# Opening order of the score and transpose steps, seeded product chains and a split last chain in a fused local-attention and squared-ReLU kernel

## The chip, the cores and the metric

The kernel runs on one core of one Trainium2 chip. The metric is the device time of one execution in microseconds (us), lower is better. Three runs of the kernel before took 202.9, 204.08 and 204.08 us; the median is 204.08 us.

## What is computed

Attention over four batches, eight heads, 768 positions and head size 64, in which a query sees the 96 latest keys and the 8 first ("global") ones, with a bias that falls with distance by a slope of its own for each head. Its output, 3072 rows of 512, goes through a two-layer network with a squared ReLU.

```python
scores = (1/8) * q @ k.T                              # per batch and head
keep   = (pos_k < 8) | ((rel >= 0) & (rel < 96))      # rel = pos_q - pos_k
dist   = where(global and not local, 96, |rel|)
a      = softmax(where(keep, scores - slope[h] * dist, -1e9))
x      = (a @ v) rearranged to (3072, 512)
out    = relu(x @ w_in) ** 2 @ w_out                  # w_in 512 x 2048, w_out 2048 x 512
```

## The kernel before, in words

**Tiles and halves.** A tile is 128 rows of one batch; six tiles make a batch, three a "half", so there are eight halves. For a tile, TensorE multiplies its queries with the keys of its own tile ("o") and with those of the tile before plus the 32 first keys ("b"). ScalarE (ACT) takes the exponential, VectorE (DVE) multiplies by a mask that holds bias and window, TensorE multiplies with v (whose 65th column of ones gives the sum), DVE divides, and the result is turned to x, columns by rows, for the first layer. In the first layer (`hps`) a job multiplies one block of 128 hidden units with the 384 rows of a half. In the second layer a pair of tiles from `layer2_pair` is multiplied by seven products instead of eight, from sums and differences of activations and weights (`token_sum`, `weight_sum`); part of the first layer does the same in `layer1_group`.

**Who decides the order.** The program lists jobs and hands them to a planner (`Plan`), a list scheduler with costs written by hand. TensorE's jobs keep the order in which they are listed, and so do the loads that GpSimd (POOL) issues. DVE and ACT operations are placed by the planner, by readiness and by `RANKS`, and then stand in a fixed order on their engine: an instruction that waits holds up everything behind it on that engine. A PSUM bank is given to a TensorE job by the planner, and comes free when its last reader is done.

**The opening** (batch 0, halves 0 and 1) is listed by hand in `OPENING` (line 20). `T r` turns q and k of tile r: eight transposes into one bank, waiting for both loads, then one copy of each; `T0` does tiles 0 and 1 in two banks. `S r o` and `S r b` are the scores of tile r. For tiles 0 to 2 the bias is added by TensorE itself: `score_tile` (line 1207) first multiplies eight scaled identities (`slope_id`) with the distance table `dmask16`, and then adds the eight products of q and k in the same two banks, so the exponential gives the weights directly (tile `ph`). `A r i` multiplies the weights with v for two pairs of heads, `X r i` turns the result to x. `V r` copies v of tile r into `vb`, with the first 32 rows replaced by the global keys; `kb` is the same for k. `F`, `G`, `E`, `D` are first-layer jobs on one, two, two and one tiles; the digit is the quarter of w_in that they need. `LOADING` (line 26) is the order of POOL's loads: q, k, v of tile r and the quarters c0 to c3 of w_in. q and k of tiles 0 and 1 come by another way: SP and ACT issue four plain loads to `y` buffers, which DVE and ACT cast.

**Fillers.** `warm` (line 274) lets TensorE multiply zeros, or turn a block of zeros, where the planner sees spare time in the first 24 us. On a bank that is to hold transposes the filler is a transpose and needs `ident`; on another it is an ordinary product of zeros.

**Chains of a pair.** In `layer2_pair` (line 1012) the products p1 and p2 make one sum, p1, p6, p7, p4 run through bank "a", p5 and p3 through "f", p2 through "c". Between them partial sums are copied out (`keep`) and added (`give`). For the last pair of all, the order is p1 p5 p6 p2 p7 p3, and then `last_part` (line 1127) does p4 in two halves of 128 columns in the same bank, each with its own copy and store.

## Time and profile before

| | |
|---|---|
| three runs | 202.9, 204.08, 204.08 us |
| the profiled execution, its own time | 203.4 us |
| its span, first to last instruction | 201.6 us |
| TensorE busy | 194.4 us (96%), 2292 products |
| weight loads of TensorE | 160.2 us (79%) |
| DVE busy | 174.6 us (87%) |
| ACT busy | 144.7 us (72%) |
| POOL busy | 67.0 us (33%) |

The profile is of one execution. Times are counted from the first instruction. "Busy" of TensorE (PE) includes the fillers and overlaps of pipelined products, so it isn't a measure of useful work. A wait is written as the engine and line that waited, an arrow, and what ended the wait. A line number can be that of a helper: L264 is every DVE copy, L262 every ACT copy, L393 every load of q, k or v. The granted TensorE clock is at full speed from 6.7 us after the start to the end.

### The profile page before, as it was taken

Reading aid. Unit: us, or ns where it says so; the run is one execution under the profiler, and the core shown is the slowest. Engines: PE = TensorE matmul, PEld = TensorE weight load, DVE = VectorE, ACT = ScalarE, POOL = GpSimd, SP = SyncE. Lnnn points to the kernel's source line nnn. Section 1 sums busy time; section 2 is a strip of 40 time slices with the busy share of each in tenths; the row PEclk is TensorE's granted clock in tenths of the full one; section 3 lists DMA queues with packets and bytes.
Section 4 is the critical chain, followed back from the end, with each engine's and each line's share of the span. In section 5 each row is a group of like instructions: output and inputs, shape, how many; then the busy total and the mean of one; then the engine's idle time right before and its main releaser. Section 6 shows DMA issues by size and latency. Waiting matters only on the chain.

```text
span 201.6 us, 5781 instructions
## 1 busy us (share of the span) xinstructions
PE 194.4 (96%) x2292; PEld 160.2 (79%) x2292; DVE 174.6 (87%) x456; ACT 144.7 (72%) x304; POOL 67.0 (33%) x82
## 2 busy tenths in 40 slices
PE   6797999999999999999999999999999999999993
PEld 6676898975797776788888878987788788987883
DVE  7679999999997699899999999989899979288922
ACT  6797989699621998978988897658886952368220
POOL 7995648169007900950491039200000000000000
PEclk9999999999999999999999999999999999999999
DMA  6999999999998998999899969995212022200123
GB/s 160 177 150 191 198 180 154 197 207 165 169 182 137 197 186 161 107 184 120 191 152 162 174 139 147 176 148 160 41 53 75 3 76 90 82 25 0 52 105 106
DMA packets 106491, 27.12 MB, mean 134 GB/s; under 512 B 96992, under 2 KB 103520, under 8 KB 106464
## 3 DMA queue, kind: packets, MB, share of 16 engines
q0 software_dynamic: 74944, 13.11, 86.2%
q1 hardware_dynamic: 30320, 13.05, 30.8%
q10 hardware_dynamic: 1200, 0.59, 1.1%
q8 instruction: 18, 0.29, 0.6%
q14 instruction: 9, 0.07, 0.1%
HBM read 27.26 MB, written 6.29 MB: 166 GB/s over the span
## 4 chain that ended last, share of the span: by engine, by line
PE 87%; DVE 4%; DMA 3%; POOL 3%; ACT 1%; issue 0%; POOLq 0%
PE yps L1025 33%; PE hps L701 27%; PE hps L804 13%; PE sp L594 4%; PE av L655 4%; PE yps L948 3%; DMA v<-in_v_dram 3%; DVE tm L1285 1%; POOL v L393 1%; POOL w_mix L393 1%; DVE vb L264 1%; PE trp L531 1%; PE av L1271 1%; DVE kb L264 1%; PE yps L1132 0%; POOL sk L393 0%
## 5 line engine op out<-in xcount | busy, mean ns | idle before, releaser
L701 PE MATMUL hps<-xt,w_in_sb 128*128 128x384 f16 (+2 forms) x432 | 62.5, 290 | 0.0
L701 PEld LDWEIGHTS <-w_in_sb 128*128 128x128 f16 x432 | 37.2, 98 | 12.1
L726 ACT ACTIVATE hr<-hps 128x384 f16<-128x384 f32 (+1 forms) x74 | 37.4, 517 | 8.5 <-PE hps L701 7.6
L262 ACT COPY y<-yps 128x256 f32<-128x256 f32 (+2 forms) x40 | 15.4, 384 | 31.3 <-PE yps L1025 26.7
L1025 PEld LDWEIGHTS <-h 128*128 128x128 f16 x344 | 32.9, 98 | 4.7
L607 ACT ACTIVATE ex<-sp 128x512 f16<-128x512 f32 x66 | 34.7, 621 | 2.7 <-PE sp L594 2.6
L393 POOL DMA_DIRECT2D sk<-in_k_dram x19 | 17.2, 914 | 51.6 <-DMA q<-sq 44.5
L1025 PEld LDWEIGHTS <-mixed 128*128 128x128 f16 x264 | 25.3, 98 | 3.4
L1080 DVE TENSOR_TENSOR y<-yps,y 128x256 f32<-128x256 f32 x33 | 13.8, 418 | 12.5 <-PE yps L1025 6.7
L393 POOL DMA_DIRECT2D v<-in_v_dram x24 | 21.6, 923 | 2.9 <-DMA w_in_sb<-in_moe_w_in_dram 1.6
L1025 PE MATMUL yps<-w_out_sb,h 128*128 128x256 f16 x176 | 21.9, 273 | 0.0
L1025 PE MATMUL yps<-w_mix,h 128*128 128x256 f16 x168 | 21.8, 273 | 0.0
L1025 PE MATMUL yps<-w_mix,mixed 128*128 128x256 f16 x176 | 21.7, 273 | 0.0
L631 DVE TENSOR_TENSOR phat<-ex,mask 128x1024 f16<-128x1024 f16 (+1 forms) x36 | 20.7, 592 | 0.1
L262 ACT COPY kept<-hps 128x384 f32<-128x384 f32 x30 | 13.4, 484 | 6.5 <-PE hps L804 6.4
L393 POOL DMA_DIRECT2D sq<-in_q_dram x19 | 16.9, 911 | 3.1 <-DVE rec L1283 1.7
L862 DVE TENSOR_TENSOR hr<-hps,kept 128x384 f16<-128x384 f32 x33 | 17.4, 547 | 0.6 <-ACT kept L262 0.3
L804 PEld LDWEIGHTS <-in_mix 128*128 128x128 f16 x176 | 14.9, 98 | 1.9
L740 ACT ACTIVATE h<-hr 128x768 f16<-128x768 f16 (+1 forms) x20 | 15.5, 775 | 0.4
L742 DVE TENSOR_TENSOR h<-hr 128x768 f16<-128x768 f16 (+1 forms) x28 | 13.9, 500 | 1.2 <-ACT hr L726 1.1
L804 PE MATMUL hps<-x_mix,in_mix 128*128 128x192 f16 x132 | 14.6, 246 | 0.0
L665 DVE TENSOR_TENSOR tm<-av,rec 128x384 f16<-128x384 f32 x24 | 13.4, 557 | 0.9
(108 smaller groups left out, 336.8 us busy)
## 6 DMA issues: line engine op xcount, KB each, us to landing
out_dram<-y SPq DMA_DIRECT2D x23, 256.0 KB, 2.4
v<-in_v_dram POOLq DMA_DIRECT2D x24, 128.0 KB, 7.1
sq<-in_q_dram POOLq DMA_DIRECT2D x19, 128.0 KB, 6.5
sk<-in_k_dram POOLq DMA_DIRECT2D x19, 128.0 KB, 5.9
w_in_sb<-in_moe_w_in_dram POOLq DMA_DIRECT2D x4, 512.0 KB, 11.1
w_out_sb<-in_moe_w_out_dram POOLq DMA_DIRECT2D x4, 512.0 KB, 10.1
y<-in_k_dram ACTq DMA_DIRECT2D x2, 256.0 KB, 4.9
y<-in_q_dram SPq DMA_DIRECT2D x2, 256.0 KB, 4.3
```

The costliest lines, as they stand in the source:

```text
L262: nc.scalar.copy(out=out, in_=in_)
L393: dma = nc.gpsimd.dma_start(out=dst, in_=src[x.b, :, r0 + t * P:r0 + (t + 1) * P, :] .rearrange("h p d -> p h d"))
L607: nc.scalar.activation(out=st["ex"][:, h], in_=sp[h], func=AF.Exp, scale=scale)
L631: eng(e).tensor_tensor(out=x.phat[a][:, :, t0:t0 + n], op=ALU.mult, in0=st["ex"][:, :, i0:i0 + 2 * n].rearrange("p e (t b) c -> p e t (b c ...
L701: nc.tensor.matmul(st["ps"][:, i * n:(i + 1) * n], lhsT=w_in_sb[:, kk, m * P:(m + 1) * P], rhs=x.xt[:, kk, c0:c1], start=kk == 0, stop=kk ...
L726: nc.scalar.activation(out=o, in_=i, func=AF.Relu)
L740: nc.scalar.activation(out=h2, in_=hr, func=AF.Square)
L742: eng(e).tensor_tensor(out=h2, in0=hr, in1=hr, op=ALU.mult)
L804: nc.tensor.matmul(st[name][:, i * HC:(i + 1) * HC], lhsT=left(i, kk), rhs=right(kk), start=fresh and i == kk == 0, stop=kk == KK - 1, ski ...
L862: eng(e).tensor_tensor(out=hidden(which)[:, :, cols], in0=sums(name), in1=st[kept], op=ALU.add)
L1025: nc.tensor.matmul(st[bank_name][:, 0:HN], lhsT=a(m), rhs=b(m), start=fresh and m == 0, stop=m == HK - 1, skip_group_check=not fresh)
L1080: eng(e).tensor_tensor(out=y, in0=ps, in1=y, op=ALU.add)
```

## The change

1. **Opening.** The bias products of tiles 0 to 2 become jobs of their own (`P r o`, `P r b`, function `distances`); `score_tile` then adds the products of q and k to the banks that these jobs took. `T r` of tiles 2 to 5 is split into `Q r` and `K r`, each with one load to wait for, four transposes, a bank of its own and one copy. `T0` and `T1` are now the two halves of what `T0` was. `OPENING` is a new order of all of it, and begins with two bias jobs; `LOADING` has a new order, too.
2. **Seeds.** Where `SEEDS` (one half of the first layer) or `PAIR_SEEDS` (three pairs of tiles) say so, the order of the seven products is p1 p5 p6 p3 p7 p2 p4: after p3 has been read out of bank "f", the sum that p1 left is copied back into that bank (`seed`), and p2 adds to it there, so p2's result is only copied or put through the ReLU instead of being added by DVE.
3. **The last pair.** Its chain p1, p6, p7, p4 runs in two banks, "a0" and "a1", each with 128 of the 256 columns: eight jobs of eight products of half the width in place of three of full width and two of half width. The last store of each half stays with SP and ACT.
4. **Constants of the planner.** `PLACES`, `MIX`, `RANKS`, `LAYER1`, `FIRST`, `KEEP`, `SHY` are changed, so jobs of the later halves stand in another order; `WIDE` does the token sums of five pairs in one piece instead of seven; `BY_DMA` makes the two v copies of the last half by DMAs that SP issues. A copy of k after its transposes comes after that of q, and the priority of some operations on ACT is changed.

```diff
-OPENING = """T0 T2 S0o S1o S2b V1 S1b A00 T3 V2 A01 S2o A10 S3o A11 A21 T4 X11 X01 S3b A20 X00 T5 X21 S4o
-X20 X10 F1 S4b A31 G11 V3 G10 G01 F0 A41 X31 A30 G00 S5b A40 F3 X30 G30 F2 X41 V4 X40 S5o
-G21 E10 E00 E11 A50 G20 A51 X50 G31 X51 E01 D0 D1"""
+OPENING = """P0o P1b T0 T1 K3 S0o K2 P1o S1b S1o Q2 A00 A01 P2b S2b P2o Q3 A10 Q5 S2o X01 A11 Q4 S3o K4
+V1 X10 A20 A21 X00 X11 S4o K5 S3b X20 X21 F1 S4b S5o G10 G11 F0 V3 V2 S5b V4 A30 G01 A40 G00
+A41 A31 X30 F3 G30 X40 X31 X41 G21 A51 A50 E11 F2 G20 G31 X51 E10 X50 E00 D0 E01 D1"""
...
-LOADING = """v1 q2 k2 k3 q3 v0 v2 q5 q4 k4 k5 c1 v3 c0 v4 c3 c2 v5"""
+LOADING = """v1 k3 k2 q3 q2 v0 q4 q5 v2 k5 k4 c1 v3 c0 v4 c3 v5 c2"""
...
-PLACES = {2: (4.0, 8.4, 10.0, 10.1, 14.3, 14.1, 0, 0, 0, 0),
...
-SHY = 0.25
-MIX = [88, 46, 22, 0, 32, 54]
-BY_DMA = [0, 0, 0, 0, 0, 0, 0, 0]
-WIDE = [1, 1, 1, 0, 1, 1, 1, 1, 0, 0, 0]
+SHY = 0.3
+MIX = [114, 48, 26, 84, 10, 70]
+BY_DMA = [0, 0, 0, 0, 0, 0, 0, 1]
+SEEDS = [0, 0, 1, 0, 0, 0, 0, 0]
+PAIR_SEEDS = [0, 0, 0, 0, 0, 1, 1, 0, 1, 0, 1]
+WIDE = [1, 1, 0, 1, 0, 0, 1, 1, 0, 0, 0]
...
-LAYER1 = {2: "ssasbsscdssessfsssg", 3: "asbcsdessfABCsgDEssFsG",
...
+LAYER1 = {2: "ssasssbsscdsesssfgs", 3: "sabcsdseAfBsCsgDEsFssG",
...
-FIRST = [0, 0, 0, 1, 2, 5, 2, 1]
-KEEP = [0, 1, 2, 1, 7, 3, 2]
+FIRST = [0, 0, 0, 1, 5, 3, 4, 1]
+KEEP = [0, 1, 2, 1, 7, 4, 3]
...
+            if seeded:
+                give(run("f", False, weight(1, 0), plain(1, 0), [ops["seed"]]), "f", 0, 0)
+            else:
+                give(run("c", True, weight(1, 0), plain(1, 0)), "c", 0, 0, "keep1")
...
-            give(job, "f", 0, 1, "keep2")
+            added = give(job, "f", 0, 1, "keep2")
+            if not seeded:
+                return
+
+            def seed(e):
+                copy(e, sums("f"), st["keep1"])
+            ops["seed"] = plan.after(job, {"ACT": 0.41, "DVE": 0.48}, seed, [added, ops["keep1"]])
+            ops["seed"].shy = {"DVE": SHY}
+            bufs["keep1"].used_by(ops["seed"])
...
+            (p1, p5, p6, p3, p7, p2, p4) if seeded else (p1, p2, p5, p6, p3, p7, p4))]
...
+            if seeded:
+                job = run("f", False, plain(x, i, 1), weight(1, 0), [ops["seed"]])
+            else:
+                job = run("c", True, plain(x, i, 1), weight(1, 0))
             x.h2_buf.used_by(job)
-            give(job, "c", 0, 0, "keep1")
+            give(job, "f" if seeded else "c", 0, 0, None if seeded else "keep1")
 
         def p5():
...
+            if seeded:
+                def seed(e):
+                    copy(e, st["f"][:, 0:HN], part(0, 0))
+                ops["seed"] = plan.after(job, {"ACT": 0.31, "DVE": 0.36}, seed,
+                                         [st["done", 0][-1], ops["keep1"]])
+                ops["seed"].shy = {"DVE": SHY}
+                y_bufs[0].used_by(ops["seed"])
 
...
-        def last_part(c):
-            cols = slice(c * HN // 2, (c + 1) * HN // 2)
-
-            def emit(e):
-                for m in range(HK):
-                    nc.tensor.matmul(st["a"][:, cols], lhsT=z.h2[:, HK + m, j * P:(j + 1) * P],
-                                     rhs=mixed_weights[0][:, 3, m, cols], start=False, stop=m == HK - 1,
-                                     skip_group_check=True)
-            job = plan.pe(HK * (HN / 4800 + 0.003), emit,
-                          [*plain(z, j, 1)[1], *mix_ops[3], ops["c22"]])
-            job.users = st["users", "a"]
-            job.users[0].append(job)
-
-            def move(e):
-                copy(e, part(1, 0)[:, cols], st["a"][:, cols])
-            op = plan.after(job, {"ACT" if c else "DVE": 0.25}, move)
...
+        def first_chain(step, c):
+            name = f"a{c}"
+            if step == 1:
+                if "s" not in st:
+                    st["s"], st["ops"] = mix_tokens(one, two)
+                job = run(name, True, plain(x, i, 0), weight(0, 0))
+                x.h2_buf.used_by(job)
+                keep(job, name, "keep1")
+            elif step == 6:
+                job = run_mixed(name, False, 1, mixed_weight(1), [ops[f"keep1{c}"]])
+                keep(job, name, "keep2")
+            elif step == 7:
+                job = run_mixed(name, False, 2, mixed_weight(2), [ops[f"keep2{c}"]])
+                give(job, name, 1, 1, "keep5")
+                ops["c22", c] = st["done", 1][-1]
+            else:
+                job = run(name, False, plain(z, j, 1), mixed_weight(3), [ops["c22", c]])
+                give(job, name, 1, 0)
+
         cost = HK * (HN / 2400 + 0.003)
         if final:
-            return [(cost, f) for f in (p1, p5, p6, p2, p7, p3)] + [
-                (cost / 2, lambda c=c: last_part(c)) for c in range(2)]
-        return [(cost, f) for f in (p1, p2, p5, p6, p3, p7, p4)]
+            def halves_of(step):
+                return [(cost / 2, lambda c=c: first_chain(step, c)) for c in range(2)]
+            return [*halves_of(1), (cost, p5), *halves_of(6), (cost, p2), *halves_of(7),
+                    (cost, p3), *halves_of(4)]
+        return [(cost, f) for f in ((p1, p5, p6, p3, p7, p2, p4) if seeded else
+                                    (p1, p2, p5, p6, p3, p7, p4))]
...
+    def turn_first(which):
+        st = first_turn
 
         def emit(e, pairs, fresh):
-            for i, src in enumerate((x.sq, x.sk)):
-                if fresh and i < n:
+            for i, src in enumerate((x0.sq, x0.sk)):
+                if fresh:
                     st[i] = bank([P, 2, NPAIR, P], FP16, "trp0", i)
                     if i == 0:
-                        warm(st[0].rearrange("p i a c -> p (i a c)"))
+                        warm(st[0].rearrange("p j a c -> p (j a c)"))
                 for a in pairs:
-                    for j in range(n):
-                        nc.tensor.transpose(out=st[i * (n - 1)][:, i if n == 1 else j, a, :],
-                                            in_=src[:, t + j, 2 * a:2 * a + 2, :], identity=ident)
-        if n == 1:
-            job = plan.pe(0.56, lambda e: emit(e, range(NPAIR), True),
-                          [x.q_in[t], x.k_in[t], ident_op], 1)
-        else:
-            half = plan.pe(0.56, lambda e: emit(e, (0, 1), True), [*first[::2], ident_op], 2)
-            job = plan.pe(0.56, lambda e: emit(e, (2, 3), False), first[1::2])
-            job.users = half.users
-            for u in job.users:
-                u.append(job)
-
+                    for j in range(2):
+                        nc.tensor.transpose(out=st[i][:, j, a, :], in_=src[:, j, 2 * a:2 * a + 2, :],
+                                            identity=ident)
...
+        if which == 0:
+            st["job"] = plan.pe(0.56, lambda e: emit(e, (0, 1), True), [*first[::2], ident_op], 2)
+            return
+        job = plan.pe(0.56, lambda e: emit(e, (2, 3), False), first[1::2])
+        job.users = st["job"].users
+        for u in job.users:
+            u.append(job)
...
+    def fix_tile(u):
+        def fix(e):
+            copy(e, batches[0].kb[:, :, u - 1, GR:P], batches[0].k[:, u, :, GR:P])
+            copy(e, batches[0].kb[:, :, u - 1, 0:GR], batches[0].k[:, 0, :, 0:GR])
+        kb_ops[u] = plan.add({"DVE": 0.65, "POOL": 1.2}, fix, [tile_ops[u][1], tile_ops[0][1]])
...
+    def turn_tile(r, i):
+        x, t = halves[r // HT], r % HT
+        st = {}
+
+        def emit(e):
+            st["ps"] = ps = bank([P, NPAIR, P], FP16, "trp0")
+            warm(ps.rearrange("p a c -> p (a c)"))
+            for a in range(NPAIR):
+                nc.tensor.transpose(out=ps[:, a], in_=(x.sk if i else x.sq)[:, t, 2 * a:2 * a + 2, :],
+                                    identity=ident)
+        job = plan.pe(0.29, emit, [(x.k_in if i else x.q_in)[t], ident_op], 1)
+        op = plan.after(job, {"ACT": 0.51, "DVE": 0.36}, lambda e: copy(
+            e, turned_to(x, i)[:, t], st["ps"]))
         x.turned.append(job)
-        for u in range(r, r + n):
-            tile_ops[u] = [evac(i, u) for i in range(2)]
-        for u in range(max(r, 1), min(r + n, NT - 1)):
-            def fix(e, u=u):
-                copy(e, bt.kb[:, :, u - 1, GR:P], bt.k[:, u, :, GR:P])
-                copy(e, bt.kb[:, :, u - 1, 0:GR], bt.k[:, 0, :, 0:GR])
-            kb_ops[u] = plan.add({"DVE": 0.65, "POOL": 1.2}, fix, [tile_ops[u][1], tile_ops[0][1]])
+        tile_ops.setdefault(r, [None, None])[i] = op
+        if i and r < NT - 1:
+            fix_tile(r)
...
+    def distances(r, before):
+        st = tiles.setdefault(r, {"weighs": []})
+        c0 = key_columns(r, before)
+
+        def emit(e):
+            st["sp", before] = pair = [bank([P, NPAIR, P], FP32, "sp", i) for i in range(2)]
+            warm(pair[0].rearrange("p a c -> p (a c)"))
+            for a in range(NPAIR):
+                for h in range(2):
+                    nc.tensor.matmul(pair[h][:, a, :], lhsT=slope_id[:, 2 * a + h, :],
+                                     rhs=dmask16[:, c0:c0 + P], start=a == 0, stop=False,
+                                     skip_group_check=True)
+        st["job", before] = plan.pe(H * (0.066 if r < 2 else 0.056), emit, slope_ops, 2)
...
-            st["sp", before] = pair = [bank([P, NPAIR, P], FP32, "sp", i)
-                                       for i in range(2)]
-            warm(pair[0].rearrange("p a c -> p (a c)"))
-            if added:
-                for a in range(NPAIR):
-                    for h in range(2):
-                        nc.tensor.matmul(pair[h][:, a, :], lhsT=slope_id[:, 2 * a + h, :],
-                                         rhs=dmask16[:, c0:c0 + P], start=a == 0, stop=False)
+            if not added:
+                st["sp", before] = [bank([P, NPAIR, P], FP32, "sp", i) for i in range(2)]
+                warm(st["sp", before][0].rearrange("p a c -> p (a c)"))
+            pair = st["sp", before]
             for a in range(NPAIR):
...
+        job = plan.pe(0.182 + NPAIR * 0.07, emit, needs, 2 - 2 * added)
+        if added:
+            job.users = st["job", before].users
+            for u in job.users:
+                u.append(job)
...
```

More of the change, by code (lines that the diff above doesn't have):

```diff
@@ L508, in fix_v @@
         else:
[L509 removed]
+            op = plan.add({"DVE": 0.62} if bt is batches[0] else {"DVE": 0.62}, values,
+                          needs, wait=0.0 if bt is batches[0] else 4.0)
+            op.shy = {"ACT": SHY}
         for t in range(t0, t1):
@@ L898, in give @@
             else:
-                done = [st["far"], done[1]]
+                done = [st["far", which], done[1]]
             def square(e):
@@ L1059, in keep @@
         def keep(job, bank_name, name):
+            cols = columns(bank_name)
+            n = cols.stop - cols.start
             def hold(e):
-                copy(e, part(*KEPT[name]), st[bank_name][:, 0:HN])
-            ops[name] = plan.after(job, {"ACT": 0.31, "DVE": 0.36}, hold)
-            y_bufs[KEPT[name][0]].used_by(ops[name])
+                copy(e, part(*KEPT[name])[:, cols], st[bank_name][:, 0:n])
+            ops[name + bank_name[1:]] = plan.after(
+                job, {"ACT": 0.1 + n * 0.00083, "DVE": 0.09 + n * 0.00105}, hold)
+            y_bufs[KEPT[name][0]].used_by(ops[name + bank_name[1:]])
         KEPT = {"keep1": (0, 0), "keep2": (0, 1), "keep5": (1, 1)}
@@ L1086, in give @@
             if final and which:
-                plan.add({"SP": 0.6}, lambda e: nc.sync.dma_start(
-                    out=out[rows[1]:rows[1] + P, HN:d_model], in_=part(1, 1)), [op])
+                if len(done) == 2:
+                    plan.add({"SP": 0.6}, lambda e: nc.sync.dma_start(
+                        out=out[rows[1]:rows[1] + P, HN:d_model], in_=part(1, 1)), done)
+                if half == 0:
+                    c = int(bank_name[1])
+                    op.costs = {"ACT" if c else "DVE": costs["ACT" if c else "DVE"]}
+                    q, queue = ("ACT", nc.scalar) if c else ("SP", nc.sync)
+                    plan.add({q: 0.6}, lambda e: queue.dma_start(
+                        out=out[rows[1]:rows[1] + P, cols], in_=part(1, 0)[:, cols]), [op])
             elif len(done) == 2:
```

105 lines of the change are left out of this document (61 added, 44 removed).

## The prediction

> **What bounds the kernel now.** I read the busy time by stretch of time first (columns: stretch, then busy time and instruction count of TensorE, its weight loads, DVE, ACT and POOL, granted clock, DMA share, GB/s).
>
> ```profile
> 6.00:10.00 4.00, 2.98 (x40) 2.46 (x39) 2.40 (x5) 2.97 (x7) 4.00 (x6) 1.00 2.43 155
> 10.00:15.00 5.00, 5.00 (x98) 4.00 (x95) 3.52 (x9) 4.57 (x9) 5.00 (x7) 1.00 2.92 150
> 15.00:20.00 5.00, 3.74 (x80) 3.06 (x74) 4.77 (x19) 3.84 (x9) 3.13 (x4) 1.00 1.60 190
> 20.00:23.00 3.00, 2.90 (x51) 2.23 (x49) 2.97 (x11) 2.98 (x8) 1.75 (x2) 1.00 1.58 193
> 23.00:60.00 37.00, 37.00 (x458) 30.18 (x457) 35.80 (x95) 28.74 (x59) 16.15 (x19) 1.00 1.75 182
> 100.00:140.00 40.00, 40.00 (x485) 33.86 (x484) 38.63 (x100) 31.24 (x68) 14.35 (x17) 1.00 1.51 159
> 185.00:198.50 13.50, 13.44 (x130) 11.93 (x128) 8.45 (x25) 4.13 (x10) 0.00 (x0) 1.00 0.19 69
> ```
>
> From 23 us to the last product TensorE never waits: 37.00 of 37.00, 40.00 of 40.00. There only its own stream can be shortened. The waits lie before 23 us, and the second view, TensorE's waits between 6 and 23 us (who waited, for what: total, times, longest), names them:
>
> ```profile
> PE sp L1227 <- DVE k L264: 1.3, 1, 1.3
> PE trp L1175 <- DMA sk<-in_k_dram: 0.5, 1, 0.5
> PE trp L1175 <- ACT sk L262: 0.4, 1, 0.4
> ```
>
> Third, the timeline around the first scores (start, length, operation, count):
>
> ```profile
> 9.71 0.40 PE L1175 MATMUL trp<-ident,sk 128*128 128x128 f16 x4 [0.51 <-DMA sk<-in_k_dram]
> 9.95 0.61 PE L1220 MATMUL sp<-early,slope_id 128*128 128x128 f16 x8
> 10.49 0.40 PE L1227 MATMUL sp<-q,k 64*128 64x128 f16 x8
> ```
>
> The first scores stand behind the load of k2, which they don't need. Eight bias products step by 0.056 us (0.45), yet the scores come 0.54 after them: going from 128-row to 64-row products costs 0.095 us, and so does going back. Last, what the chain of waits shows before TensorE is fully fed:
>
> ```profile
> 6.34 0.85 POOL v L393
> 7.19 6.26 DMA v<-in_v_dram
> 13.48 0.63 DVE vb L264
> 14.13 0.84 DVE vb L264
> 15.09 0.42 DVE tm L1285
> ```
>
> It runs over a load of v and then DVE until 21.3 us. So the opening is bound by loads first, then by DVE, not by TensorE alone.
>
> **Part 1, the opening.** Up to the job F1, both orders hold the same TensorE jobs, and before starts F1 at 20.84. What counts is when F1 starts now. I walk it with durations of before.
>
> TensorE starts with eight zero products 512 wide at about 1.2 instead of 41 transposes at 1.67. Those step by 0.107 us while the clock is low, so 512 columns are about 0.43 each (estimate: four times), to 4.6. The scaled identities are ready at 4.5, so the 16 bias products run to 6.3. The last cast of k in the first tiles ends at 7.53 in any order, so the first transposes end at 8.0 as before. The 16 bias products thus cost nothing, and take 16 x 0.056 = 0.9 us off what follows. If that cover fails they cost the same 0.9 where they stand.
>
> K3 now needs the second load (landed 8.77); the first scores follow at 9.2 instead of 10.49. But ACT then has the copies of K3 and K2 (0.48 us a step each) ahead of and between the exponentials, and a copy of q5: ten exponentials, which ended at 16.30, end at about 16.6. DVE gets kb of three tiles early, vb of tile 1 until 13.4 (v0, the sixth load in both orders, landed 12.40), the norms A00 and A01, the copy of q3 and A10 until 15.5. Then stands vb of tile 2. It waits for v2, now ninth in line; the ninth load of before landed at 16.33. Everything behind it on DVE waits too: A11 and both norms of tile 2, whose results TensorE needs for X20 and X21. From 16.4: vb 0.8 at most, xt 0.25, A11 0.6, two copies 0.75, A20 and A21 1.1: 19.9. Meanwhile TensorE waits for K4, whose load is eleventh (17.42). X20 and X21 then come at 20.0, and F1 at 20.05.
>
> F1 also needs c1, twelfth in both orders, and this is a floor:
>
> ```profile
> L454 POOL DMA_DIRECT2D w_in_sb<-in_moe_w_in_dram x4: 747/830/855, 11.5 to 16.6; - x4
> DMA to landing us min/median/max: 8.4/11.1/12.6
> ```
>
> The first quarter, issued 11.5, landed 8.4 later, at 19.9; the last, issued 16.6, 12.6 later, at 29.2. So F1 gains 20.84 - 20.05 = 0.8 us, and at most 0.9.
>
> The next floor is c2: it moves from 17th to 18th in line, and the 18th load landed at 30.3. Before, c2 is first needed by F2, at 30.24. Now G21 needs it: 9.4 us of work from F1 on as before, less 0.27 of gaps after F1 in before, plus S5o (0.22), X40 and X41 (0.22), and 0.2 for the copies of X20 and X21, which stand behind kb and two mask products on DVE. That is 20.05 + 9.77 = 29.8; it waits till 30.35. There it has done 0.22 + 0.22 + 0.19 (two changes of row count saved, since S4b and S5o run together) = 0.63 more than before at 30.24: ahead by 0.52 us. Were c2 not late, it would be 1.05.
>
> The trace has no row for copies of DVE under the new order, and they are its weak point: vb took 0.84 us at 12.5, while POOL wrote descriptors without a break (5.00 of 5.00 above), and 0.28 at 26.4, when POOL waited. I take 0.8 for vb of tile 2 as one slow and one fast piece; two slow pieces make 0.9 more than two fast ones. The Trainium skill, "SBUF — State Buffer", section on who interferes with whom, says why: DVE copies in a two-port mode and GpSimd's descriptor writing shut each other out completely. By that rule kb of tile 3, now at 10.0, must run slow, and vb of tile 2 runs fast if POOL waits at 16.4; the trace agrees as to the copies. It makes the first rival below.
>
> **Part 2, seeds.** Three pairs and one group in the first layer. Each takes an addition from DVE (0.42 or 0.55) and adds a copy (0.37 or 0.48), mostly on ACT. p2 now waits for drain, addition and copy: 0.2 + 0.42 + 0.37 and two hand-overs, some 1.2 us after p3 (1.4 in the first layer); TensorE's later jobs queue behind p2. In the new order TensorE has p7 and other jobs between p3 and p2: 0.87 + 0.78 (twelve pairs of scores), 0.65 + 0.87 + 0.33, and far more in the third pair; 2.9 in the first layer. Cost zero; without that cover 0.3 to 0.5 each.
>
> **Part 3, the last pair.** The tail before:
>
> ```profile
> 197.38 1.06 PE L1132 MATMUL yps<-w_mix,h 128*128 128x128 f16 x16
> 198.48 0.29 DVE L264 COPY y<-yps 128x128 f32<-128x128 f32 x1 [0.40 <-PE yps L1132]
> 198.80 0.27 ACT L262 COPY y<-yps 128x128 f32<-128x128 f32 x1 [3.47 <-DVE y L264]
> 199.10 0.37 ACTq L1144 DMA_DIRECT2D out_dram<-y  x1
> ```
>
> The copy of the first half waits until the second half's products are done, and ACT's copy waits for DVE's: one bank. With two banks ACT copies at 198.48: 0.32 earlier, and the last store, which ACT issues, goes with it. 16 half-width products take 0.89 against 0.87 for eight: three more steps, 0.06. Each half step has at least 1.3 us of other products before the next of its chain, so no wait. Net -0.26.
>
> **Part 4, the constants.** TensorE's work is the same; DVE's is not. Counting forms by their rows: four more ReLUs of 384 columns (2.4), three narrow ones (0.5), other copies and split token sums (1.4) against two vb pairs (1.1), additions and copies of x (2.2): about +1.0 us on 174.6. Forecast zero, if it falls where DVE has room; otherwise 1.0 late or more, which is the last rival. SP's four new DMAs are ahead of three transposes of the half before; the v loads they wait for landed by 133, and those transposes come near 139, so nothing waits.
>
> **The sum.** -0.52 - 0.26 = -0.8 us on a span of 201.6: 200.8, and with the 1.8 us around it 202.6. That is on the profiled execution's 203.4; the median of the runs shown, 204.08, lies 0.7 above it, the lowest, 202.9, 0.5 below.
>
> **Rivals.**
> - *Copies shut out (first part hidden).* DVE's vb and kb run slow at 16.4 to 18: F1 0.9 later, near before's. For: POOL's remaining loads fall there. Against: it sat idle for 1.0 us at 15.6. Only the tail and 0.2 of row changes stay: 203.0.
> - *Loads land sooner.* From the ninth load on, one of the 16 engines was 1.3 us behind the other 15, after a 16 KB instruction fetch of 1.5 us at 13.4. TensorE now reaches that instruction count nearly 1 us later. If v2, k4 and c1 escape it, F1 is bound by the walk without v2's wait, 0.9 sooner, and c2 comes at 29: gain 1.7 in all, 201.7.
> - *DVE becomes the bound in the middle (slower).* At 100 to 140 us DVE is busy 38.63 of 40. The new orders put 1.0 us more on it, and what is late there holds up all behind it, so two or three such delays can add up; if they come to more than the 0.8 gained, TensorE waits for squares and token sums in front of `hps` and `yps` jobs: between 203.4 and 205, some 204.2. Against: at nearly the same share of DVE before shows no wait in 175 us.
>
> **How the numbers follow.** Forecast 0.50, copies shut out 0.15, loads sooner 0.20, DVE-bound 0.15. The range takes in loads sooner with the bound of its cost and most of DVE-bound: 200.9 to 204.4. One per cent of the median is 2.04 us, about what a measurement of this kernel can tell from no change; three runs already spread by 1.2. Under 202.04: half of loads sooner, a quarter of the forecast: 0.23. Over 206.1: less than half of DVE-bound: 0.06. The rest, 0.71.
>
> **What would show it.** Right: first scores near 9.2, DVE waiting for v2 near 16, F1 near 20 just behind c1, a wait before G21, no wait after 31, ACT's last copy straight after the last product. Wrong: F1 after 20.6 with DVE copies of 0.6 to 0.8 before it; a wait of TensorE for DVE after 40 us; F1 at 19.3 with c1 landed before 19.

## The result, and the profile after

The changed kernel took 204.89 us (median of 17 runs, 203.6 to 205.76), the kernel before beside it 203.59 us (17 runs, 202.6 to 204.86). The ratio is 1.0059, 95% interval 1.0034 to 1.0084: 1.2 us slower, where 0.8 us faster was forecast. The profiled execution took 204.75 us, and its span went from 201.6 to 203.0 us. The first page of its profile, and the row of TensorE's busy tenths:

```profile
span 203.0 us, 5797 instructions
PE 194.7 (96%) x2288; PEld 157.6 (78%) x2288; DVE 175.1 (86%) x461; ACT 145.9 (72%) x310; POOL 66.7 (33%) x82
PE   7887999999999999999989999999999999999993
```

The work is the same. DVE has 0.5 us more of it, TensorE does 0.3 us more in a span that is 1.4 longer. The busy time by stretch (columns as before) says where TensorE stood still:

```profile
6.00:10.00 4.00, 3.26 (x53) 2.50 (x51) 2.45 (x6) 3.69 (x9) 4.00 (x6) 1.00 2.42 154
10.00:15.00 5.00, 4.45 (x89) 3.64 (x86) 4.46 (x14) 4.37 (x10) 5.00 (x7) 1.00 2.88 148
15.00:20.00 5.00, 3.95 (x83) 2.97 (x78) 3.98 (x16) 4.00 (x10) 3.10 (x4) 1.00 1.61 191
23.00:60.00 37.00, 36.64 (x455) 29.86 (x453) 35.15 (x91) 29.15 (x61) 16.33 (x20) 1.00 1.74 182
60.00:100.00 40.00, 39.62 (x447) 29.70 (x445) 34.18 (x90) 30.89 (x64) 16.54 (x19) 1.00 1.63 160
100.00:140.00 40.00, 39.48 (x475) 32.89 (x473) 38.95 (x102) 32.80 (x70) 15.01 (x18) 1.00 1.51 155
140.00:185.00 45.00, 45.00 (x485) 37.76 (x482) 39.13 (x96) 29.23 (x63) 0.00 (x0) 1.00 0.19 56
```

The stretches from 23 to 140 us, where TensorE was never idle in the execution shown of before, now lose 0.36, 0.38 and 0.52. The middle one of before:

```profile
60.00:100.00 40.00, 40.00 (x456) 30.67 (x455) 35.22 (x91) 31.82 (x66) 17.69 (x20) 1.00 1.54 162
```

From 140 to 185 us, when the loads are over, nothing is lost. TensorE's waits from 23 us on, by who ended them:

```profile
PE sp L599 <- DVE tm L670: 0.5, 1, 0.5
PE hps L706 <- DMA w_in_sb<-in_moe_w_in_dram: 0.4, 1, 0.4
PE hps L706 <- DMA xt<-tm: 0.2, 1, 0.2
```

The second is the wait for c2 that was forecast; the other two were not. This view counts idle time only. Measured from the start of a product to the start of the next, against the step of its shape, the trace has 0.52 at 29.5 us, 0.39 at 69.2, 0.31 at 71.4, 0.14 at 87.8, 0.12 at 97.6, 0.68 at 101.5 and 0.29 at 192.5 us.

The opening went as it was walked. First the longest waits from 6 to 23 us (for K4's load, the casts and the load of q2), then, from the timeline, the first scores, at 9.07 instead of 10.49:

```profile
PE trp L1269 <- DMA w_mix<-in_k_dram: 1.0, 1, 1.0
PE trp L1232 <- ACT sk L264: 0.5, 1, 0.5
PE trp L1269 <- DMA sq<-in_q_dram: 0.4, 1, 0.4
```

```profile
9.07 0.40 PE L1312 MATMUL sp<-q,k 64*128 64x128 f16 x8
```

F1 starts at 19.92, just behind c1 (landed 19.87). The tail, with a wait ahead of the last pair, is the whole of the new chain of waits, since it ends in TensorE's own wait at 192.8:

```profile
192.83 0.04 issue
192.87 6.79 PE yps L1053 x88
199.66 0.02 issue
199.69 0.27 ACT y L264
```

**A measure for what follows.** The lead of an execution at a moment is how much less TensorE still had to do there than in the execution shown of before: the time from that moment to the end of the last product, less the start-to-start waits after it, taken from the same figure of before. It is worked out from the start times in each trace, of one execution each. A lead that falls has been spent on waits.

| us | 40 | 60 | 73 | 89 | 93 | 104 | 150 | 194 |
|---|---|---|---|---|---|---|---|---|
| changed kernel | 0.73 | 0.73 | 0.02 | -0.12 | -0.12 | -0.92 | -0.92 | -1.21 |
| changed, second execution | 0.94 | 0.94 | -0.16 | -0.50 | -0.50 | -1.42 | -1.43 | -1.72 |
| before, second execution | 0.59 | 0.59 | 0.58 | 0.59 | 0.59 | 0.02 | 0.02 | 0.02 |
| only the last pair | 0.42 | 0.41 | 0.41 | -0.06 | -0.06 | -0.41 | -0.41 | -0.69 |
| only the opening | 0.54 | 0.54 | 0.54 | -1.23 | -1.23 | -1.47 | -1.37 | -1.47 |
| only constants, seeds | -0.23 | -0.23 | -0.23 | -0.23 | -0.23 | -0.27 | -1.47 | -1.47 |
| later loads | 0.95 | 0.95 | 0.95 | 0.24 | 0.24 | -0.10 | -0.10 | -0.38 |
| fewer loads | 0.93 | 0.93 | -1.30 | -1.30 | -1.30 | -1.30 | -1.30 | -1.59 |
| fewer and later loads | 0.64 | 0.64 | 0.64 | 0.64 | 0.64 | 0.63 | 0.64 | 0.35 |
| before, fewer loads | 0.73 | 0.73 | 0.73 | 0.73 | 0.73 | 0.29 | 0.29 | 0.29 |

### The profile page after: what moved, and what is told of

Its sections match the earlier page's. It is cut to its first block, busy times and chain, and to the rows that moved or that the text cites. A ratio compares the mean times of both kernels' runs of the same rounds, so it can differ in the third digit from the quotient of the medians.

```text
span 203.0 us, 5797 instructions
## 1 busy us (share of the span) xinstructions
PE 194.7 (96%) x2288; PEld 157.6 (78%) x2288; DVE 175.1 (86%) x461; ACT 145.9 (72%) x310; POOL 66.7 (33%) x82
## 2 busy tenths in 40 slices
DMA packets 106812, 27.39 MB, mean 135 GB/s; under 512 B 97057, under 2 KB 103841, under 8 KB 106785
## 5 line engine op out<-in xcount | busy, mean ns | idle before, releaser
L731 ACT ACTIVATE hr<-hps 128x384 f16<-128x384 f32 (+1 forms) x71 | 36.9, 529 | 9.8 <-PE hps L706 9.1
L1053 PEld LDWEIGHTS <-h 128*128 128x128 f16 x376 | 34.3, 98 | 4.8 <-issue 0.2
L264 ACT COPY y<-yps 128x256 f32<-128x256 f32 (+1 forms) x45 | 16.5, 368 | 29.4 <-PE yps L1053 29.0
L1053 PE MATMUL yps<-w_mix,h 128*128 128x256 f16 (+1 forms) x192 | 22.9, 264 | 0.1
L1053 PE MATMUL yps<-w_out_sb,h 128*128 128x256 f16 (+1 forms) x184 | 22.2, 268 | 0.0
L1053 PE MATMUL yps<-w_mix,mixed 128*128 128x256 f16 (+1 forms) x184 | 21.4, 268 | 0.0
L1115 DVE TENSOR_TENSOR y<-yps,y 128x256 f32<-128x256 f32 (+1 forms) x31 | 12.7, 409 | 10.1 <-PE yps L1053 5.9
L636 DVE TENSOR_TENSOR phat<-ex,mask 128x1024 f16<-128x1024 f16 (+1 forms) x36 | 20.2, 595 | 0.0
```

Source lines behind the costliest of these rows:

```text
L264: nc.scalar.copy(out=out, in_=in_)
L636: eng(e).tensor_tensor(out=x.phat[a][:, :, t0:t0 + n], op=ALU.mult, in0=st["ex"][:, :, i0:i0 + 2 * n].rearrange("p e (t b) c -> p e t (b c ...
L731: nc.scalar.activation(out=o, in_=i, func=AF.Relu)
L1053: nc.tensor.matmul(st[bank_name][:, 0:n], lhsT=a(m), rhs=b(m)[:, cols], start=fresh and m == 0, stop=m == HK - 1, skip_group_check=not fresh)
```

## The experiments

Ratios are to the kernel before, run on the same chip, with 95% intervals.

**1. Later loads.** In the trace of after, POOL's loads for two halves ahead begin at 59.84 us (before: 61.89), because their buffers are free sooner: the transpose of q landed at 59.28 instead of 61.34. The last two transposes of x, issued by SP at 61.39 and 62.73, then land at 67.42 and 69.74 (before: 63.67 and 66.24). TensorE and DVE stand there:

```profile
69.78 0.97 PE L706 MATMUL hps<-xt,w_in_sb 128*128 128x384 f16 x5 [0.23 <-DMA xt<-tm]
69.86 0.36 DVE L788 TENSOR_TENSOR x_mix<-xt,x_mix 128x384 f16<-128x384 f16 x1 [1.69 <-DMA xt<-tm]
```

A second suspect was the copy of k in front of the wait at 101.5 us: 1.05 for the two pieces at 99.47, with POOL writing descriptors from 99.22 on; in before 0.62 at 97.43, with POOL idle.

In this edit `x.hb` is the half that is loaded, `prev.xturns` are the transposes of x of the half two before it.

```diff
+                if x.hb in (4, 6) and name == "sk" and t == 0:
+                    behind(dma, prev.xturns[{4: 1, 6: 0}[x.hb]])
```

> The changed kernel, its instructions in the same order on every engine; only two groups of GpSimd's loads start later: those that began at 59.8 us wait for the second transposing DMA of x of that stretch, those that began at 99.2 us wait for the first. Theory (two collisions): the wait for x at 69 us (0.39, and 0.31 behind it at 71 us) comes from transposes of x that share the DMA engines with these loads, and the 0.68 at 101.5 us from a DVE copy of k that took 0.89 instead of 0.45 beside descriptor writing. Then the x transposes land in under 4.5 us after issue instead of up to 7.0, the copy of k takes about 0.45, both waits go, and the time falls by 1.0 to 1.4 us against the changed kernel, to about 203.6 (ratio to the kernel before 0.998 to 1.002). Rival (DVE has more work): the waits stay or move, since DVE's work is the same, and the time stays at 204.9 (ratio 1.006). Rival (later loads are late themselves): a new wait for q or k appears 15 us behind each, and the time is above 204.9.

Measured: 204.90 us, 1.0072 (1.0045 to 1.0099). The time did not move, yet the waits did, in a profiled execution that was the shortest of the twelve (203.92): x landed at 63.45 and 65.86, and nothing is lost at 69 to 71. The copy of k took 0.62 instead of 1.05. DVE came to it at 99.37 instead of 99.47, 0.10 apart, and to the operation that ends the wait at 101.5 us at 100.77 instead of 101.66, 0.89 apart. Of the 0.80 lost between 93 and 104 us 0.34 is left, nearly all of it at 97.3. The lead of 0.95 lived until 87 us, and was spent there, again on x, whose last part landed at 87.74:

```profile
87.79 0.82 PE L708 MATMUL hps<-xt,w_in_sb 128*128 128x384 f16 x4 [0.55 <-DMA xt<-tm]
```

So both mechanisms are right for their places, and were not what set the time.

**2. One part at a time.** "Only the opening" has the new `OPENING`, `LOADING` and turns with the constants and the last pair of before; "only constants, seeds" has those alone; "only the last pair" the two banks alone. The planner lays out all later work anew in the first two. The edit of the first, against the changed kernel, in its core (the others are parts 2 and 4, and part 3, of the change put on the kernel before):

```diff
-SHY = 0.3
+SHY = 0.25
...
-SEEDS = [0, 0, 1, 0, 0, 0, 0, 0]
+SEEDS = [0, 0, 0, 0, 0, 0, 0, 0]
...
-            return [*halves_of(1), (cost, p5), *halves_of(6), (cost, p2), *halves_of(7),
-                    (cost, p3), *halves_of(4)]
+            return [(cost, f) for f in (p1, p5, p6, p2, p7, p3)] + [
+                (cost / 2, lambda c=c: last_part(c)) for c in range(2)]
```

> The kernel before with the new opening and order of loads alone: no seeds, the constants and the last pair of before. Theory (the opening gains what was forecast, the loss is elsewhere): F1 starts near 19.9, a wait for c2 of about 0.5 near 30, then at most 0.3 of waits; 0.4 to 0.8 us faster than the kernel before (ratio 0.996 to 0.998). Rival (being early moves the loads and transposes of the middle against each other whatever the constants): waits of 0.3 or more after 40 us, and a ratio of 1.000 to 1.004.

Measured: 204.96 us, 1.0074 (1.0042 to 1.0107). F1 at 19.91 and 0.52 for c2 came as forecast; then, as the rival had it, 0.81 and 0.68 at 87 to 89 us, and a time above even the rival's. SP's queue had put two transposes of x ahead of q's, q's landed at 62.83, the next loads began at 63.45, and the last part of x landed at 89.18.

> The kernel before with the new constants and the seeds alone: opening and last pair of before. Theory (the new constants make the waits): TensorE, which never waited there, waits 0.8 to 1.7 us between 40 and 190 us, and the time is 0.8 to 1.7 us above the kernel before (ratio 1.004 to 1.008). Rival (the waits come from the opening's shift): no wait above 0.2 us in the middle, ratio 0.999 to 1.001.

Measured: 205.31 us, 1.0085 (1.0043 to 1.0127). TensorE loses 0.94 at 109 us. DVE shows why: it stands 1.40 for x, and the addition that TensorE waits for stands behind it.

```profile
108.76 0.36 DVE L788 TENSOR_TENSOR x_mix<-xt 128x384 f16<-128x384 f16 x1 [1.40 <-DMA xt<-tm]
...
109.97 0.42 DVE L1115 TENSOR_TENSOR y<-yps,y 128x256 f32<-128x256 f32 x1
...
110.44 1.03 PE L1053 MATMUL yps<-w_mix,h 128*128 128x256 f16 x8 [0.78 <-DVE y L1115]
```

> The kernel before with the last pair's chain in two banks alone. The forecast's step: 0.26 us faster, ACT's last copy straight behind the last product, no wait ahead of it. Theory from the trace of the changed kernel: the last product of the pair before this one now has 0.39 us of other products ahead of it instead of 0.87 and waits about 0.3 for DVE's addition; ACT's copy is 0.3 earlier, but the last store of SyncE lands last instead, so that only 0.1 of it is left: in all 0.1 to 0.4 us slower (ratio 1.000 to 1.002).

Measured: 204.04 us, 1.0029 (1.0006 to 1.0052), with 0.29 at 192.0 us. The half-width first step (0.45 of products) now stands where the whole step (0.87) stood ahead of the last product of the pair before. In the changed kernel:

```profile
192.13 0.61 PE L1053 MATMUL yps<-w_out_sb,h 128*128 128x128 f16 x8
...
192.40 0.42 DVE L1115 TENSOR_TENSOR y<-yps,y 128x256 f32<-128x256 f32 x1
...
192.87 1.03 PE L1053 MATMUL yps<-w_mix,h 128*128 128x256 f16 x8
```

DVE's addition ends at 192.82, and the product needs it; the half step in front of it is through at 192.57.

The opening and the constants are each, alone, as slow as all together, and the last pair costs 0.6, so the costs don't add. What "only the last pair" showed besides is the clue: up to 185 us it has the instructions of before in the same order, and still its F1 is at 19.97, not 20.84, it waits 0.49 at 31.6 and 0.48 at 87.5, and its last part of x lands at 88.04.

**3. Both kernels again.**

> The kernel before, unchanged: one more execution to look at. Theory (the base of the forecast was one draw): with the same instructions the copies of vb on DVE between 12.5 and 15 us take another time whenever they fall otherwise beside GpSimd's descriptor writing: F1 starts anywhere between 19.9 (c1's landing) and 20.9, and where it starts near 19.9 the lead of 0.9 is spent by 90 us: on c2 near 30 (0.3 to 0.6) and on the last transposed part of x near 88 (landed 87.3 to 88.1 in four of the five plans looked at so far, 89.2 in the other). Rival: F1 at 20.8 and no wait of TensorE up to the end, as in the execution shown before.

Measured: 203.38 us, span 201.6, F1 at 19.85, and the last product ends at 198.42 (198.44 in the execution shown before). The lead of 1.0 at F1 was gone by 100 us: 0.13 for c2 and 0.49 for a copy of x at 29 to 32 us, 0.42 and 0.15 at 95 to 99. Not x at 88 this time (landed 87.23) but v: DVE came to its copy of v 0.5 us earlier than in the first execution, and waited that much longer for the same landing.

```profile
91.69 0.61 DVE L264 COPY vb<-v 128x520 f16<-128x520 f16 x2 [0.87 <-DMA v<-in_v_dram]
```

```profile
91.70 0.61 DVE L264 COPY vb<-v 128x520 f16<-128x520 f16 x2 [0.35 <-DMA v<-in_v_dram]
```

The first is the second execution, the other the one that the prediction was made on. The lead itself came from DVE's copies of v in the opening, three pieces, in the second execution and in the first:

```profile
12.37 0.28 DVE L264 COPY vb<-v 32x520 f16<-32x520 f16 x1 [0.48 <-DMA v<-in_v_dram]
13.34 0.68 DVE L264 COPY vb<-v 128x520 f16<-128x520 f16 x2 [0.68 <-DMA v<-in_v_dram]
```

```profile
12.50 2.47 DVE L264 COPY vb<-v 32x520 f16<-32x520 f16 x3 [0.53 <-DMA v<-in_v_dram]
```

The pieces took 0.29, 0.29 and 0.35 against 0.84, 0.62 and 0.84, with POOL writing descriptors all the while in both. Of six traces with the old opening, four had the quick copies and F1 at 19.72 to 19.97 (at c1's landing), two the slow ones and F1 at 20.84 and 20.90.

> The changed kernel, unchanged: one more execution. If its waits belong to its plan, F1 is again at 19.8 to 20.0, with about 0.5 for c2 near 30, 0.1 to 0.7 at 87 to 88 us, 0.5 or more between 97 and 103 us and 0.29 at 192 us. If they are chance, they lie elsewhere and only the 0.29 stays.

Measured: 205.27 us: 0.52 at 29.3, 0.80 and 0.31 at 69 to 72, 0.34 at 88.0, 0.51 at 98.1, 0.24 at 102.5, 0.29 at 193.0. In these two executions the waits belong to the plan in their places, not in their sizes.

**4. Mends.** `after_mended` makes three groups of loads wait (at 59.8, 80.6 and 99.2 us) and puts both half steps ahead of the product; `pair_mended` and `after_pair_mended` do the latter, and split a store, on before and on after.

```diff
+LATER = {(4, 'sk', 0): 1, (5, 'sk', 0): 1, (5, 'sk', 2): 2, (5, 'sq', 1): 3, (6, 'sk', 0): 0}
...
+                if (x.hb, name, t) in LATER:
+                    behind(dma, prev.xturns[LATER[x.hb, name, t]])
...
-                main[-1:] = [jobs[0], *last, *jobs[1:]]
+                n = 2 if hb == NHB - 1 else 1
+                main[-1:] = [*jobs[:n], *last, *jobs[n:]]
...
+            elif final:
+                plan.add({"SP": 0.6}, lambda e: nc.sync.dma_start(
+                    out=out[rows[0]:rows[0] + P, half * HN:(half + 1) * HN],
+                    in_=part(0, half)), [op])
```

> The changed kernel with its order kept but for one job, and three edits: GpSimd's loads that began at 59.8, 80.6 and 99.2 us wait for transposes of x (of the group at 80.6 the first load for the second of them, the third load for the third, the fifth for the last), and the last pair's first step goes as a whole, not as a half, ahead of the last product of the pair before. Theory (x's last part, landed at 88.0, takes the lead): x lands by 86.5, the wait at 87 to 88 us goes, with it those at 69, 71 and 101 us and the 0.29 at 192 us; what is left of waits after 31 us is 0.3 to 0.5 us of the 1.9; 203.0 to 203.9 us (ratio to the kernel before 0.996 to 1.002). Rival (DVE's work bounds the middle): the waits come back for squares and token sums, 204.4 or more (ratio 1.004 or more). Rival (the loads are then late): waits for q or k near 100 us, above 205.

Measured: 204.84 us, 1.0084 (1.0064 to 1.0104): no gain. Its profiled execution took far longer than its median (span 206.0), so no sizes are taken from it. Holding loads back alone gained nothing in either run; where this one loses the time is not shown.

> The kernel before with the last pair in two banks and two mends: both halves of its first step ahead of the last product of the pair before (0.89 us of products there instead of 0.45), and the store of the last row tile but one split in two, the first half issued about 1.7 us earlier. Theory: the 0.29 us wait at 192 us goes, SyncE's last store has 128 KB less in front of it and lands with ACT's, 0.3 to 0.6 us earlier than in the kernel before, less 0.06 for half-width products: 0.2 to 0.5 us faster than the kernel before (ratio 0.9975 to 0.999). Rival (the landing of the last store is set by the issue on SyncE, one more store makes it later): as the kernel before or slower, 1.000 to 1.002.

Measured: 203.40 us, 1.0016 (0.9999 to 1.0034). The wait at 192 us is gone, and the last store lands 1.95 us after the last product instead of 2.27. But the span still ends 3.31 after it (before: 3.19). So the rival's time came, for another reason, told in the last section.

> The changed kernel with the two mends of the last pair alone (both halves of its first step ahead of the product before, the store of the last row tile but one split). Theory: the 0.29 us wait at 192 us goes and the stores land 0.1 to 0.3 earlier behind the last product: 0.3 to 0.6 us faster than the changed kernel, 204.3 to 204.6 (ratio to the kernel before 1.003 to 1.006). Rival: the wait is not from the halved cover and stays; ratio 1.006 to 1.008.

Measured: 204.56 us, 1.0043 (1.0019 to 1.0066): 0.3 us under the changed kernel's 204.89, at the low end of what was expected. The 0.29 is gone, and 0.99, 0.31 and 0.51 at 69, 72 and 102 us remain.

**5. Fewer loads.** The same order of work on every engine, but POOL leaves out a third of the loads from 59.8 us on; the transposes of these halves then wait for the last load of k. The decisive run is the third.

```diff
             def emit(e):
+                if name == "sq" and x.hb >= 4:
+                    return
...
-                    in_=getattr(x, name).rearrange("p t h d -> p (t h d)"))
+                    in_=(x.sk if x.hb >= 4 else getattr(x, name)).rearrange("p t h d -> p (t h d)"))
```

> The changed kernel without the 12 loads of q for the last four halves (from 59.8 us on, a third of the loads there); q is transposed from k's tile instead, so the output is another one. The rest is in the same order on every engine. Theory (loads and transposes pace TensorE up to about 105 us, so that a lead is spent waiting for x): k and q are turned some 3 us earlier, the last part of x lands by 86 instead of 88.0, TensorE's lead of 0.7 to 0.9 us at 60 us is still above 0.3 at 110 us (it was -0.9 and -1.4), and the time falls by 0.8 to 1.5 us to 203.4 to 204.1. Rival (DVE, or the order of the work, bounds the stretch): DVE's work is the same, the lead at 110 us is again below -0.7, and the time stays within 0.4 of 204.9.

Measured: 203.90 us, 1.0019 (0.9991 to 1.0047): 1.0 under the changed kernel (0.8 by the ratios). No wait above 0.1 from 74 to 192 us; but 1.86 and 0.31 at 69 to 73, where the first loads still fall beside the last transposes of x (landed 71.13). This execution, at 205.15 us, was one of the longest of twelve, and its lead at 110 us is the -1.30 of the table, not above 0.3 as expected. The time is the theory's, the lead of this one execution the rival's, so this run alone decides nothing.

> The kernel before without the same 12 loads. Theory (loads and transposes pace it too): an execution with F1 near 19.9 keeps its lead of 0.5 to 0.6 past 100 us, where the second look at this kernel lost it, and the median falls by 0.2 to 0.6 us to about 203.0. Rival: as the kernel before, ratio 0.999 to 1.001.

Measured: 203.31 us, 0.9973 (0.9954 to 0.9993). That is within what was expected. The profiled execution took 510 us, so its trace shows nothing here; the other eleven lie between 202.93 and 203.45, where the kernel before beside it spreads from 202.65 to 204.84.

> The changed kernel without the 12 loads of q (q from k's tile, another output), and with the loads that began at 59.7 us waiting for the second transpose of x, as in the first experiment; order of work unchanged. Each edit alone moved the wait: later loads took away the 1.1 at 69 to 71 us and the lead went at 87 us; fewer loads took away those at 86 to 104 us and the lead went at 69 us. Theory (the lead is lost only to x landing late beside loads): with both, no wait above 0.15 us between 31 and 190 us, a lead of 0.6 to 0.9 us over the execution of before at 110 us, 0.29 lost at 192 us, and 202.8 to 203.3 us (ratio to the kernel before 0.995 to 0.998; the rest of the forecast's gain). Rival (the new order has waits of its own on DVE): waits come up at other places, lead at 110 us below 0, 203.8 or more (ratio 1.001 or more).

Measured: 203.20 us, 0.997 (0.9949 to 0.9991), 202.86 to 203.33 in twelve runs. Its stretches:

```profile
23.00:60.00 37.00, 36.64 (x454) 29.86 (x453) 35.13 (x90) 29.27 (x61) 16.20 (x19) 1.00 1.74 182
60.00:100.00 40.00, 40.00 (x456) 30.67 (x454) 35.60 (x95) 32.17 (x68) 15.90 (x18) 1.00 1.30 153
100.00:140.00 40.00, 40.00 (x478) 33.12 (x476) 39.06 (x101) 32.85 (x71) 5.34 (x6) 1.00 1.13 129
140.00:185.00 45.00, 45.00 (x485) 38.03 (x483) 39.16 (x96) 28.74 (x62) 0.00 (x0) 1.00 0.17 50
```

Only c2's 0.36 is left of the idle time. The lead of 0.64 goes unspent from 40 to 190 us, with DVE at 39.06 of 40 from 100 to 140 us, as busy as in the changed kernel. The copy of k takes 1.24 at 98.04 here, beside descriptor writing, and TensorE doesn't wait: here a slow copy costs nothing.

> The kernel before without the 12 loads of q, a second look, since the profiled execution of the first was of no use. Theory: where F1 starts near 19.9, the lead of 0.5 to 0.6 us at 60 us is still there at 110 us, and the time is 202.8 to 203.2. Rival: it is lost at 87 or 95 us as in the kernel before, 203.4.

Measured: 203.13 us, F1 at 19.72. The lead of 0.73 held past 87 us, 0.44 of it went at 98.9 behind DVE, and 0.29 reached the end, where the full kernel kept 0.02. DVE has no gap there from a slow copy of k to the addition that TensorE waited for (before, with all loads: 0.62 for that copy):

```profile
96.69 1.31 DVE L264 COPY kb<-k 128x1152 f16<-128x1152 f16 x2
...
98.77 0.55 DVE L864 TENSOR_TENSOR hr<-hps,kept 128x384 f16<-128x384 f32 x1
```

So a slow copy costs time where DVE has none to spare. The two kernels now stand level: 0.997 for the changed one with fewer and later loads, 0.9973 for before with fewer. The one is 0.35 ahead of the other at 150 us, and loses 0.43 around the last pair. Even with room for the loads no gain of the change is shown.

## Why the prediction was wrong, point by point

**The step that failed** is the first: "From 23 us to the last product TensorE never waits", and with it the sum, which carried the lead won in the opening to the end. No wait of TensorE in one execution was read as room on every other engine. It was a coincidence of two paces. The page of before had the other in sight, the busy tenths of its DMA engines in 40 slices of 5 us:

```profile
DMA  6999999999998998999899969995212022200123
```

They are taken nearly without a break for 27 slices, to 136 us. Loads feed the transposes of q and k, these free the buffers of the next loads, and x's transposes share the engines with those; so x and v land late even where TensorE is early. The last part of x of one half landed at 87.76 in before, and at 87.23, 88.04, 88.03, 88.42, 87.74 and 89.18 in before's second execution, the last pair alone, after, its second execution, the later loads and the opening alone, whose leads at 60 us run from 0.41 to 0.95. Only in before's second execution did x come sooner with the lead; there v did not (landed 91.66 against 91.68). The middle of after took 1.65 (0.73 at 40 us to -0.92 at 104); without a third of the loads and with one group later, it takes nothing. That edit takes away packets and POOL's descriptor writing together. At 69 and 87 us TensorE waits for x itself, whose transposes SP issues; at 97 to 102 us the two are not told apart.

One row of the profile may bear on how full they are: over nine tenths of the DMA packets of after are under 512 B (97057 of 106812). The Trainium skill, "DMA: Bandwidth & Descriptors", Specifications, gives 512 B as the least size for full rate. No run here changed the size of a packet, so this is not shown as the cause.

**Part 1** was right in its steps: scores at 9.07 (forecast 9.2), DVE waiting for v2 until 16.31, F1 at 19.92 (20.05), c2's wait 0.52 (0.55). The lead after it was 0.73 (0.52). Its base was not: F1 at 20.84 was one draw of two. Over the six executions with the old opening the mean lead at 60 us is 0.34, over the seven read with the new 0.80; the opening gains about 0.5, and not the 0.8 of the walk; beside the four old openings with quick copies it gains some 0.2.

The copies forecast as one slow and one fast piece were both fast (0.30 and 0.28). The rule of the Trainium skill, "SBUF — State Buffer", section on who interferes with whom, that the two-port copies of DVE and GpSimd's descriptor writing shut each other out, agrees with the slow draws (0.84 against 0.28). The section adds that whoever issues first keeps the ports for its whole instruction, and two of the three pieces of the second execution passed at full speed within writing that had begun before them; so the rule did not foretell which copies are slow here. The trace that the prediction was made on already had such a one: a copy of v at 11.69 took 0.28 beside unbroken writing.

Two rivals fell with it: no copy of 16 to 18 us was shut out, and no load came sooner (v2 at 16.29, c1 at 19.87, c2 at 30.00, against 16.33, 19.93 and 30.32 for the same places in line).

**Part 2**, seeds at zero: right where the loads leave room. In the run with fewer and later loads all four seeds stand, and TensorE is never idle between 31 and 190 us.

**Part 3** was wrong by 0.7: forecast -0.26, traced +0.29 and +0.14 in the tail. The covers were counted within the pair; the one outside it, the last product of the pair before, was missed: 0.29. ACT's copy did follow the last product at once (199.69):

```profile
198.59 1.06 PE L1053 MATMUL yps<-w_mix,h 128*128 128x128 f16 x16
...
199.24 0.29 DVE L266 COPY y<-yps 128x128 f32<-128x128 f32 x1
...
199.69 0.27 ACT L264 COPY y<-yps 128x128 f32<-128x128 f32 x1 [3.27 <-PE yps L1053]
...
199.98 0.36 ACTq L1133 DMA_DIRECT2D out_dram<-y  x1
```

Its store was issued 0.33 sooner behind the last product, but landed only 0.08 sooner (2.19 against 2.27), right behind two others, and more was checked after it (last section). With the part alone the tail is 3.05, 0.14 shorter than before, so there the trace has 0.15 against the part; it measured 0.6 slower (0.1 to 1.1), with the lead lost in the middle as well.

**Part 4**, forecast zero, is where the middle's 1.65 stands, and the rival "DVE becomes the bound in the middle" got the sign and nearly the time (204.2). The sign that it gave, a wait of TensorE for DVE after 40 us, came too (0.5 at 101.5). Half of its mechanism held: what is late on DVE holds up all behind it. The other half fell: DVE has 0.5 more, not 1.0, and with the same work on DVE the waits go when the loads make room. DVE passes on what comes late: x or v, and around 100 us a copy of k that took 1.05 beside descriptor writing. The new constants do cost time under the full loads: 1.7 us (0.9 to 2.6) by themselves, 0.94 of it traced to a late x.

**The span** adds up: -0.73 for the opening, +1.65 in the middle, +0.29 ahead of the last pair, +0.14 in the tail (3.33 against 3.19 us after the last product) make +1.35, and 1.4 was measured. Of the middle's 1.65, 0.68 stands behind the slow copy of k and went when that took 0.62. The sizes at 97 to 102 us changed between two executions of one kernel, and how much of them is the copy and how much the late v ahead of it stays open.

No version here beats the kernel before on its full work; `pair_mended` comes level with it.

## What to carry to other kernels

An engine without a wait in one profile may just be keeping step with another pace: before a gain at the start is carried to the end, look for what does not land sooner in between (here loads and transposes on full DMA engines), and ask how late its next user comes. Take the base of an opening from several executions where the same copy can take 0.3 or 0.8 us. When a step is cut in two, recount the cover of every job that stood behind the whole of it, in the neighbouring chains too.

## What was not expected of the hardware

The same three copies of v on DVE, in the same order and beside the same unbroken descriptor writing, took 0.93 us in one execution and 2.30 in another, and F1 moved by 1.0 us with them.

The spread from run to run depends on the loads: in the kernel before, 12 fewer of them narrowed it from 2.2 us (202.65 to 204.84, 29 runs) to 0.5 (202.93 to 203.45, eleven runs). In the changed kernel the same edit left 2.1 (203.13 to 205.2), and 0.5 came only when x also landed in time (202.86 to 203.33).

After the last store SyncE checks the DMA semaphores one after another, 0.06 us each, in an order that does not follow the landings. In before the last store's was the last of the list, 0.92 us from the end of the span; in after four remained behind it (1.14), in `pair_mended` seven (1.35), which took back more than the 0.32 that its stores landed sooner.
